# A gate with key sums on half the array, strided fills in place of mask tables, and a new written order of all steps

## The chip, the cores and the metric

The kernel runs on one core of one Trainium2 chip. Its metric is the device time of one execution in microseconds (us). The core has five engines that run side by side and wait for each other by semaphores: TensorE (PE, with weight loads shown apart as PEld), VectorE (DVE), ScalarE (ACT), GpSimd (POOL) and SyncE (SP), which here does nothing but issue DMAs. Each engine takes its own instructions strictly in the order in which the program wrote them, so one that waits holds up all that stand behind it on that engine. PSUM, where TensorE writes, is used as four places of 4 KB per partition.

## The reference, cut to what matters

Two layers follow one another. The first is a block-sparse attention over 4 batches, 8 heads, 768 positions and 64 features. The second mixes its output by a two-dimensional Fourier transform (real part) and ends in a normalised two-layer network.

```python
k_rep = k.reshape(B, H, n_blocks, block, D).mean(axis=3)      # 12 blocks of 64 keys
gate_scores = np.einsum('bhsd,bhnd->bhsn', q, k_rep)
gate_scores = np.where(causal, gate_scores, -1000000000.0)
top_idx = np.argsort(gate_scores, axis=-1)[..., -top_k:]      # top_k = 3
# a query may see the keys of its three best blocks and of its own block, causally
scores = np.where(mask, scale * (q @ k.T), -1000000000.0)
x = softmax(scores) @ v                                       # heads side by side: (4, 768, 512)
mixed = np.real(np.fft.fft(np.fft.fft(x, axis=1), axis=2))
u = x + mixed
un = (u - mean(u)) / sqrt(var(u) + 1e-6)
out = u + maximum(un @ w_ch1, 0.0) @ w_ch2                    # 512 -> 2048 -> 512
```

## The kernel before, in words

The work is cut into 16 pairs of heads (four pairs to a batch) and then into four batches. The text `ORDER` names every step by letters and indices, and a loop at the end of the kernel (L767) writes the steps' instructions in exactly that order. Every engine's queue is therefore `ORDER` with the other engines' steps left out. Nothing is reordered later.

**Loads** (SP's queue): `Lk`, `Lq`, `Lv` fetch a pair's keys, queries and values into `nat` buffers (three for k, three for q, two for v); pairs 7 to 15 have k and q fetched by four DMAs in blocks of 32. `LF`, `LT`, `Lc`, `Li` fetch Fourier and indicator tables. `W:c` and `X:c` fetch the network's weights and are issued on POOL's queue.

**Attention of a pair P.** For P below 7 (`NX`), `tk` and `tq` transpose k and q on PE into PSUM; from 7 on, `kb` and `qc` transpose 32x32 blocks on DVE. `ks` (DVE, L306) sums keys by block into `kr12`; `kh` (DVE, recorded at the helper of all two-operand steps, L221) multiplies these sums by a table `half` of 0 and 1, so that each of the two heads has sums on its own 64 partitions and zeros on the other 64. `kc` (ACT) and `qc` (DVE), `qs` (POOL) make the copies that the score matmuls read. The **gate** is `g` (PE, block scores: L347 or L354), `gt` (DVE: turn the scores, then shut out blocks that lie ahead: for P below 7 a minimum with the table `lim`, else three fills), `gx` (DVE: the eight largest of each row), `gl:P,0` (DVE: 1 where a block is below the third largest), `gl:P,1` (DVE: multiply by the table `oth` or `oth2`, which holds -60000 or, for the own block, 0) and `gm` (DVE: turn back, giving `mt`). For P from 7 on, `K` (POOL, ten instructions) copies `mt` beside the queries. `s` (PE, six tiles 0 to 5) makes the scores with the mask added, by the indicator rows `indz` in matmuls of their own (L433) for P below 7, or within the same matmul of 96 rows (L426). `e` (ACT, L443) takes the exponential, `d` (POOL, L449) clears the upper triangle of the diagonal part, `vc` (POOL) casts v, `v` (PE, L461) multiplies by v, `x` (DVE, L472 and L221) divides by the sum.

**Fourier part and network of a batch b.** `fs`, `fd`, `f` (DVE) fold the batch's four pairs; `pg` (POOL) holds POOL until the folds are done. `y` (PE), `ty` (ACT) and `tr` (DVE), `m` (PE, three), `u` (DVE, L578, adds x), `xu` (ACT, centres) follow. The result is turned by `xt` (PE) and `un` (DVE, L602) for batch 0 and by six DMAs on SP's queue for the others (`un`, L605). Then come 16 steps `w` (PE, L641 and L643, first layer) with `r` (ACT or, every fourth, DVE), and 12 steps `c` (PE, L668) with `o` (DVE, L680) and `od` (SP, the output). `bn`, `nv` (DVE) and `nr` (POOL) make the norm.

**PSUM and other buffers.** All PSUM tiles share one tag with four buffers, which are handed out in turn: a new tile waits until the tile four allocations earlier has been read. `nat`, `q32`, `mt`, `pt` and `u_b` rotate in the same way.

Before the first `w` there is no network work with which to fill PE; from then on `w` and `c` steps of one batch stand between the attention steps of the next.

Of the kernel before, what the change touches and what calls it, by code (L numbers as in the profile page):

```python
# [11 lines left out]
FP = mybir.dt.float32  # L12
# [3 lines left out]
NEG = -60000.0  # L16
# [12 lines left out]
def _consts_np():  # L29
# [22 lines left out]
    oth = np.where(np.arange(9)[:, None] + 3 != nn, NEG, 0.0)[None].repeat(128, 0)  # L52

    lim = np.where(nn[None, 4:8] > np.arange(3, 7)[:, None], -3e38, 3e38)
    lim = lim.reshape(1, 16).repeat(128, 0).astype(np.float32)
# [6 lines left out]
    own = 2 * np.arange(5)[None, :] + 2 + (p // 64)[:, None]  # L62
    oth2 = np.zeros((128, 5, 2, 16), np.float32)
    oth2[:, :, :, 0:NB] = np.where(own[:, :, None, None] != nn, NEG, 0.0)
# [3 lines left out]
    return dict(FS=fs.astype(np.float16), FD=fd.astype(np.float16),  # L68
                oth=oth.reshape(128, 108).astype(np.float16),
                lim=lim,  # L70
                indc=indc.reshape(128, 24).astype(np.float16),
                oth2=oth2.reshape(128, 160).astype(np.float16),
# [40 lines left out]
Lk:1 Lq:1 Lk:2 Lq:2 Lq:3 Lk:3 tk:0 ks:0 kh:0 iz:1 iz:0 tq:0 kc:0 qc:0 g:0 tq:1 gt:0 gx:0 gl:0,0  # L113
gl:0,1 gm:0 qc:1 tk:1 kc:1 tk:2 kc:2 ks:1 qs:0 qs:1 Lq:4 Lv:0 Lk:4 Lv:1 kh:1 s:0,1 ks:2 s:0,3 tq:2
qc:2 g:1 kh:2 e:0,1 s:0,0 s:0,5 gt:1 s:0,4 s:0,2 tk:3 e:0,3 e:0,5 g:2 gx:1 gl:1,0 Lq:5 Lk:5 gl:1,1
gm:1 s:1,4 tq:3 s:1,3 e:0,0 tq:4 gt:2 tk:4 e:0,4 ks:3 qc:3 gx:2 gl:2,0 s:1,0 kh:3 qc:4 gl:2,1 s:1,1
e:0,2 g:3 ks:4 e:1,4 gm:2 Lv:2 d:0,3 qs:2 d:0,4 d:0,2 vc:0 vc:1 d:0,0 d:0,1 d:0,5 Lv:3 Lq:6 LF:0
Lq:7 Lk:6 Lk:7 LT:0 v:0 s:1,5 s:2,4 e:1,3 kc:3 tq:5 e:1,0 s:2,5 s:2,2 e:1,1 gt:3 kc:4 gx:3 gl:3,0
kh:4 x:0 e:1,5 g:4 s:1,2 s:2,3 e:2,4 e:2,5 qc:5 gl:3,1 e:2,2 gt:4 e:1,2 tk:5 gx:4 gm:3 ks:5 e:2,3
s:2,1 e:2,1 qs:4 qs:3 vc:2 d:1,4 d:2,5 qs:5 d:1,0 d:1,3 d:1,5 d:1,2 d:1,1 fs:0,0 kh:5 gl:4,0 fs:0,1  # L120
gl:4,1 v:1 x:1 s:3,1 s:2,0 s:3,4 g:5 kc:5 s:3,3 e:3,1 e:3,4 s:3,0 qc:7 gm:4 e:2,0 tq:6 e:3,0 s:3,5
e:3,5 e:3,3 gt:5 s:3,2 s:4,1 e:3,2 fs:1,1 gx:5 fs:1,0 gl:5,0 Lv:4 Lq:8 Lk:8 Lv:5 Lc:0 d:3,1 d:2,1
d:2,2 d:3,4 d:2,0 d:3,5 d:3,0 d:2,3 d:2,4 vc:3 d:3,2 d:3,3 gl:5,1 kb:7 v:2 e:4,1 kc:7 gm:5 ks:7 v:3
s:4,5 e:4,5 s:4,0 qc:6 x:2 s:5,4 e:5,4 s:5,5 s:4,4 x:3 s:5,2 s:4,3 s:5,0 tk:6 e:5,5 fs:2,0 kh:7
fs:3,1 fs:3,0 fs:2,1 fd:3,0 fd:2,0 fd:2,1 fd:3,1 f:0,2 f:0,0 f:0,1 y:0,0 e:4,4 ks:6 f:0,3 y:0,1
e:5,2 s:5,3 e:5,0 e:4,0 tr:0,0 e:4,3 tr:0,1 m:0,2 kc:6 ty:0,0 g:7 ty:0,1 kh:6 m:0,1 u:0,2 g:6 u:0,1
# [3 lines left out]
r:0,6 w:0,12 e:6,1 w:0,11 w:0,2 qc:8 ks:8 gm:7 kb:9 kh:8 g:8 r:0,12 s:6,0 r:0,11 s:6,5 w:0,0 e:6,4  # L130
r:0,2 w:0,5 w:0,8 w:0,1 e:6,5 ks:9 r:0,5 gt:8 gx:8 gl:8,0 kh:9 gl:8,1 w:0,3 bn:0,5 gm:8 qc:9 bn:0,3
Lq:10 Lk:10 Lv:6 Lq:11 d:6,1 K:7 qs:7 d:6,4 d:5,2 d:5,4 d:6,3 X:0 d:5,3 d:6,5 d:5,5 vc:5 d:5,1 Li:0
Lv:7 Lq:12 Lv:8 Lv:9 s:7,3 v:5 r:0,8 r:0,0 r:0,3 r:0,1 e:6,0 bn:0,1 x:5 s:7,2 e:7,3 w:0,15 g:9 s:7,4
e:7,2 w:0,9 e:7,4 fs:5,0 s:7,5 gt:9 s:7,1 w:0,13 r:0,15 r:0,9 s:7,0 kb:10 gx:9 ks:10 qc:10 kh:10
fs:4,1 w:0,10 gl:9,0 fs:5,1 g:10 w:0,14 e:7,1 e:7,5 e:7,0 w:0,7 bn:0,4 gt:10 bn:0,0 bn:0,2 gx:10
gl:9,1 gm:9 r:0,7 r:0,13 w:0,4 gl:10,0 gl:10,1 nv:0 d:6,0 qs:8 K:8 X:1 d:7,4 d:6,2 d:7,0 d:7,2 d:7,5
vc:7 d:7,1 vc:6 qs:9 d:7,3 K:9 nr:0 v:6 kc:8 s:8,5 s:8,2 r:0,14 s:8,4 r:0,10 kc:9 v:7 r:0,4 c:0,0,0
s:9,0 s:8,3 s:9,1 e:8,5 c:0,0,1 s:9,3 x:6 x:7 c:0,1,0 s:8,0 e:8,2 fs:6,1 c:0,1,1 fs:7,1 fs:7,0
fd:7,0 fs:4,0 fs:6,0 fd:6,0 qc:11 fd:7,1 fd:6,1 f:1,2 f:1,0 f:1,3 f:1,1 y:1,0 tr:1,0 e:8,4 e:8,3
o:0,1 e:9,1 kc:10 e:9,3 y:1,1 c:0,4,0 e:9,0 e:8,0 c:0,5,0 ty:1,1 s:8,1 o:0,0 Lv:10 Lv:11 Lk:11 Lq:13  # L140
od:0,1 od:0,0 Lq:14 Lk:12 ty:1,0 s:9,5 e:9,5 tr:1,1 kb:11 ks:11 kh:11 m:1,1 m:1,0 g:11 e:8,1 u:1,1
# [658 lines left out]
```

## Time and profile before

| what | value |
|---|---|
| median of 3 runs | 293.21 us (292.3 to 293.62) |
| the profiled execution: span from first to last instruction | 290.3 us |
| PE / DVE / ACT / POOL busy | 274.3 / 203.0 / 164.4 / 113.2 us |
| TensorE clock granted | 1.000 of full speed |
| bytes read / written | 28.63 MB / 6.29 MB |

The profile states the profiled execution by its span alone. The three runs lie 2.0 to 3.3 us above that span, which is the time around the first and the last instruction together with the difference between executions; a change in the span is carried over to the time as it stands.

How to read it: an engine's busy time says how much of the span it worked, not whether it set the end. The view by stretches gives the busy time of each engine in a stretch. The view of waits says who waited for whom. The chain that ended last goes from the last instruction back to whatever released each step. In views of one tile or line the three durations are the least, the median and the largest in nanoseconds.

### The profile page before, as it was taken

How to read it: one execution, taken by the hardware profiler on the slowest of the kernel's cores; microseconds unless marked ns; L12 is line 12 of the kernel's file. 1: busy time of each engine (PE TensorE's matmuls, PEld its weight loads, DVE VectorE, ACT ScalarE, POOL GpSimd, SP SyncE). 2: the span in 40 equal slices, each digit the busy share in tenths (PEclk: the TensorE clock that was granted, in tenths of full speed). 3: DMA queues.
4: the chain of work that ended last, by engine and by line, in shares of the span. 5: the costliest groups of instructions: out<-in, count | busy, mean ns of one | idle time of the engine just before them, and what ended most of it. 6: DMA issues, size and time to landing. Idle time of an engine off the chain costs nothing.

```text
span 290.3 us, 6581 instructions
## 1 busy us (share of the span) xinstructions
PE 274.3 (94%) x2525; PEld 167.7 (58%) x2525; DVE 203.0 (70%) x606; ACT 164.4 (57%) x205; POOL 113.2 (39%) x286
## 2 busy tenths in 40 slices
PE   7696976899999999999999999999999999999995
PEld 3554664575656665565576457646766654656443
DVE  2899988999789988689988668609691559202122
ACT  3676878877579666579888505687143231263000
POOL 2246470614988815845760489414400001100000
PEclk9999999999999999999999999999999999999999
DMA  9999999899999399964900004541000024000034
GB/s 200 267 236 263 172 215 178 140 180 162 154 189 205 76 183 212 130 131 117 213 17 2 0 0 148 109 92 73 2 2 0 36 76 108 0 2 0 0 147 181
DMA packets 121423, 33.52 MB, mean 115 GB/s; under 512 B 114160, under 2 KB 118192, under 8 KB 121392
## 3 DMA queue, kind: packets, MB, share of 16 engines
q1 hardware_dynamic: 115728, 28.47, 46.0%
q0 software_dynamic: 3664, 4.19, 9.2%
q10 hardware_dynamic: 2000, 0.44, 0.7%
q8 instruction: 20, 0.33, 0.5%
q14 instruction: 11, 0.09, 0.1%
HBM read 28.63 MB, written 6.29 MB: 120 GB/s over the span
## 4 chain that ended last, share of the span: by engine, by line
PE 79%; DVE 13%; ACT 5%; issue 2%; DMA 1%; DVEq 0%; ACTq 0%
PE c L668 27%; PE h L641 19%; PE h L643 10%; PE sc L426 7%; PE av L461 4%; ACT pt L443 4%; DVE u L578 2%; PE yp L531 2%; DVE kr L306 2%; DVE q L328 2%; PE warmps L705 1%; PE sc L421 1%; DVE mx L378 1%; PE c L660 1%; PE g L354 1%
## 5 line engine op out<-in xcount | busy, mean ns | idle before, releaser
L443 ACT ACTIVATE pt<-sc 128x1024 f16<-128x1024 f32 (+1 forms) x96 | 83.5, 918 | 26.1 <-PE sc L426 14.6
L641 PE MATMUL h<-unT,w 128*128 128x512 f16 x256 | 84.5, 379 | 0.0
L668 PE MATMUL c<-w_sb,hT 128*128 128x512 f16 x368 | 83.0, 379 | 0.2 <-ACT pt L443 0.2
L643 PE MATMUL h<-unT,w 128*128 128x256 f16 x256 | 69.7, 272 | 0.0
L449 POOL TENSOR_SCALAR_AFFINE_SELECT pt<-pt 128x256 f16<-128x256 f16 x96 | 38.5, 424 | 68.0 <-ACT pt L443 45.9
L668 PEld LDWEIGHTS <-hT 128*128 128x128 f16 x368 | 35.7, 98 | 40.6 <-issue 0.7
L653 ACT ACTIVATE hT<-h 128x768 f16<-128x768 f32 x48 | 37.4, 809 | 34.7 <-PE h L643 34.6
L641 PEld LDWEIGHTS <-w 128*128 128x128 f16 x256 | 25.0, 98 | 29.5 <-issue 0.7
L680 DVE SCALAR_TENSOR_TENSOR u<-c,rs,u 128x512 f32<-128x512 f32 (+1 forms) x25 | 17.3, 724 | 29.9 <-PE c L668 25.6
L651 DVE TENSOR_SCALAR hT<-h 128x768 f16<-128x768 f32 x16 | 15.2, 948 | 19.4 <-PE h L643 19.4
L643 PEld LDWEIGHTS <-w 128*128 128x128 f16 x256 | 25.0, 98 | 3.9
L426 PE MATMUL sc<-qk 96*128 96x512 f16 (+3 forms) x144 | 26.0, 306 | 0.1
L224 POOL TENSOR_SCALAR_AFFINE_SELECT qk<-q 64x768 f16<-64x768 f32 (+1 forms) x25 | 21.0, 843 | 12.8 <-DVE q L328 12.1
L590 ACT ACTIVATE x<-u,nm 128x512 f16<-128x512 f32 x24 | 16.0, 714 | 16.3 <-DVE nm L584 16.2
L224 POOL TENSOR_SCALAR_AFFINE_SELECT qk<-mt 32x160 f16<-32x160 f16 x72 | 23.0, 340 | 2.6 <-DVE mt L398 0.9
L461 PEld LDWEIGHTS <-pt 128*128 128x128 f16 x672 | 22.2, 97 | 2.8 <-issue 1.1
L461 PE MATMUL av<-v,pt 128*128 128x65 f16 x672 | 23.0, 193 | 0.5 <-ACT pt L443 0.3
L421 PE MATMUL sc<-qk 64*128 64x512 f16 (+3 forms) x112 | 14.9, 306 | 5.4 <-ACT pt L443 3.2
L578 DVE SCALAR_TENSOR_TENSOR u<-mx,x 128x512 f32<-128x512 f32 x24 | 15.6, 685 | 5.2 <-PE mx L565 5.2
L224 POOL TENSOR_SCALAR_AFFINE_SELECT v<-nat 128x768 f16<-128x768 f32 x16 | 14.7, 920 | 8.6 <-DMA nat<-in_v_dram 8.6
L426 PEld LDWEIGHTS <-qk 96*128 96x128 f16 x144 | 12.7, 97 | 8.6 <-issue 0.9
L544 ACT CAST ty<-yp 128x772 f16<-128x772 f32 x8 | 8.0, 1036 | 16.7 <-PE yp L531 16.4
(98 smaller groups left out, 349.2 us busy)
## 6 DMA issues: line engine op xcount, KB each, us to landing
nat<-in_v_dram SPq DMA_DIRECT2D x16, 384.0 KB, 5.0
out_dram<-u SPq DMA_DIRECT2D x23, 256.0 KB, 2.5
nat<-in_q_dram SPq DMA_DIRECT2D x36, 96.0 KB, 3.0
nat<-in_k_dram SPq DMA_DIRECT2D x36, 96.0 KB, 3.1
nat<-in_k_dram SPq DMA_DIRECT2D x13, 192.0 KB, 3.3
nat<-in_q_dram SPq DMA_DIRECT2D x13, 192.0 KB, 3.5
w_sb<-in_moe_w_ch_dram POOLq DMA_DIRECT2D x2, 1024.0 KB, 9.8
w<-in_moe_w_ch_dram POOLq DMA_DIRECT2D x2, 768.0 KB, 9.4
```

The lines of the kernel that those rows point to most:

```text
L224: nc.gpsimd.affine_select(out=out, in_=in_, pattern=[[0, i] for i in n], base=0, channel_multiplier=0, compare_op=ALU.is_ge, fill=0.0)
L421: nc.tensor.matmul(ps[:, e, co:co + q1 - q0], qk[hs[e], 1, XW(P), 128 * jt:128 * jt + 128], qk[hs[e], 0, XW(P), q0:q1], start=(co == 0), s ...
L426: nc.tensor.matmul(ps[:, e, co:co + q1 - q0], qk[0:96, e, 1, 128 * jt:128 * jt + 128], qk[0:96, e, 0, q0:q1], start=True, stop=True)
L443: nc.scalar.activation(out=d["pt"][:, o:o + 2 * n].rearrange("p (e c) -> p e c", e=2), in_=d["sc", i][:, :, 0:n], func=AF.Exp, scale=0.125)
L449: nc.gpsimd.affine_select(out=dg, in_=dg, pattern=[[0, 2], [1, 128]], base=0, channel_multiplier=-1, compare_op=ALU.is_ge, fill=0.0)
L461: nc.tensor.matmul(av[:, e, 66 * st:66 * st + 65], pt[:, co:co + 128], vv[:, e, jt, 0:65], start=(cnt == 0), stop=(cnt == 20))
L578: nc.vector.scalar_tensor_tensor(out=u_b[:, k2, :].rearrange("p (m two) -> p two m", two=2), in0=mps[:, k2, :].rearrange("p (two m) -> p t ...
L641: nc.tensor.matmul(hp[:, 0:512], w1s, unT[:, dt, 0:512], start=(dt == 0), stop=(dt == NDT - 1))
L643: nc.tensor.matmul(hp[:, 512:768], w1s, unT[:, dt, 512:768], start=(dt == 0), stop=(dt == NDT - 1))
L653: nc.scalar.activation(out=hT, in_=hp, func=AF.Relu)
L668: nc.tensor.matmul(c_ps[b, g[0]][:, st - g[0], :], h_t[b, it][:, 128 * st:128 * (st + 1)], w2_sb[:, it, :], start=(it == 0), stop=(it == N ...
L680: nc.vector.scalar_tensor_tensor(out=o, in0=ps, scalar=st_t[b][1][:, st:st + 1], in1=o, op0=ALU.mult, op1=ALU.add)
```

## The change

Six things are done together.

1. **Key sums (pairs 0 to 6).** `kh` is dropped for these pairs. `ks` writes `kr_s` directly; its second head axis is gone. The gate's matmul reads only the 64 partitions of its head, `kr_s[hs, :]` against `qq[hs, ...]`, so each matmul uses half the array's rows.
2. **Block bound (pairs 0 to 6).** The minimum with `lim` becomes two strided fills of `gt` with -3e38.
3. **Own block.** The product with `oth` or `oth2` is dropped. A new step `go` fills the own block's score with 3e38 after `gx` (one fill for P below 7, two from 7 on), so that it is never below the third largest. `gl` is now one instruction.
4. **Masks.** They are 0 and 1. The -60000 moves into the indicator tables `indc` and `ind`.
5. **Tables.** `lim`, `oth` and `oth2` and their three loads (two on ACT's queue at the start, one in `Lc` on SP's) are gone.
6. **Order and places.** `ORDER` is written anew from start to end, and steps carry `@n`. PSUM tiles and the rotating buffers have one tag for each place n with one buffer each. A tile now waits for the last tile of its place, whatever was allocated in between.

```diff
     for g in range(4):
         for n in range(NB):
-            indc[g, n, g % 2, n] = 1.0
+            indc[g, n, g % 2, n] = NEG
...
-        ind[e, 16 * e:16 * e + NB] = nn[:, None] == (s[None, :] // 64)
+        ind[e, 16 * e:16 * e + NB] = np.where(nn[:, None] == (s[None, :] // 64), NEG, 0.0)
...
-    psump = ctx.enter_context(tc.tile_pool(name="psum", bufs=4, space=bass.MemoryType.PSUM))
+    psump = ctx.enter_context(tc.tile_pool(name="psum", bufs=1, space=bass.MemoryType.PSUM))
...
+    place = [0]
+
     def pst(shape, name, dtype=FP):
-        return psump.tile(shape, dtype, tag="ps", name=name)
+        return psump.tile(shape, dtype, tag=f"ps{place[0]}", name=name)
...
-    kr_s = [ctile([128, 2, 32], FP, f"kr{i}") for i in range(NSLOT)]
+    kr_s = [ctile([128, 32], FP, f"kr{i}") for i in range(NSLOT)]
...
     def a_sums(P):
         ps = pairs[P]["tp", 1]
-        pairs[P]["kr12"] = kr12 = spool.tile([128, NB], FP, tag="kr12", name=f"kr12_{P}")
+        if P < NX:
+            kr12 = kr_s[P % NSLOT][:, 0:NB]
+        else:
+            pairs[P]["kr12"] = kr12 = spool.tile([128, NB], FP, tag="kr12", name=f"kr12_{P}")
...
             for c in range(4):
+                hs = slice(64 * (c // 2), 64 * (c // 2) + 64)
                 nc.tensor.matmul(g[32 * c:32 * c + 32, :].rearrange("p (b i) -> p b i", i=32),
-                                 kr_s[slot][:, c // 2, :], qq[:, :, c % 2, :], start=True, stop=True)
+                                 kr_s[slot][hs, :], qq[hs, :, c % 2, :], start=True, stop=True)
...
             nc.vector.transpose(out=gt, in_=d["g"])
-            x = gt.rearrange("p (b n) -> p b n", n=32)[:, 0:4, 4:8]
-            tt(x, x, lim, ALU.min)
+            for c, n in ((4, 4), (6, 2)):
+                nc.vector.memset(gt[:, c:c + 33 * n].rearrange("p (b n) -> p b n", n=33)[:, :, 0:2],
+                                 -3e38)
             return
...
-        if j == 0:
-            tt(l, gt, mx[:, :, 2:3].to_broadcast([128, 9 if P < NX else 10, NB]), ALU.is_lt)
-        else:
-            tt(l, l, o, ALU.mult)
+        tt(l, gt, mx[:, :, 2:3].to_broadcast([128, 9 if P < NX else 10, NB]), ALU.is_lt)
+
+    def g_own(P):
+        gt = pairs[P]["gt"]
+        if P < NX:
+            nc.vector.memset(gt[:, 3:3 + 33 * 8 + 1:33], 3e38)
+            return
+        for h in range(2):
+            nc.vector.memset(gt[64 * h:64 * h + 64, 2 + h:2 + h + 170].rearrange(
+                "p (b c) -> p b c", c=34)[:, :, 0:17:16], 3e38)
...
         for x in ORDER.split():
+            x, _, at = x.partition("@")
+            place[0] = int(at or 0)
             n, a = x.split(":")
             WORK[n](*[int(i) for i in a.split(",")])
```

Of the order, the stretch around the first `w` before, then the new one there and at the hand-over to batch 1:

```diff
-s:4,2 gt:6 e:5,3 m:0,0 s:5,1 xu:0,2 e:4,2 xu:0,1 xt:0,1 gx:6 e:5,1 u:0,0 xu:0,0 Lk:9 Lq:9 W:0 W:1
-d:4,0 pg:0 vc:4 d:4,4 d:5,0 qs:6 d:4,3 d:4,1 W:2 d:4,2 d:4,5 gl:6,0 gl:6,1 v:4 un:0,1 gm:6 s:6,3
-gt:7 xt:0,0 xt:0,2 s:6,1 s:6,4 x:4 e:6,3 s:6,2 e:6,2 un:0,0 un:0,2 gx:7 gl:7,0 gl:7,1 kb:8 w:0,6
...
+e:5,4 s:5,5@2 f:0,0 e:5,5 s:5,0@1 e:4,1 tk:6@2 f:0,1 f:0,2 e:5,0 y:0,0@0 Lk:9@2 ks:6 f:0,3 kc:6
+y:0,1@1 tr:0,0 pg:0 d:4,4 Lk:8@1 vc:6 g:6@2 tr:0,1 ty:0,0 qs:6 qc:7@0 ty:0,1 m:0,2@0 W:1 gt:6
+Lv:5@1 e:5,2 m:0,0@1 d:5,0 u:0,2@0 d:5,5 Lc:0 m:0,1@2 d:5,4 W:2 g:7@3 u:0,0@1 xu:0,2 vc:4 xt:0,2@0
+d:4,5 d:5,1 u:0,1@2 xu:0,0 d:4,1 d:4,3 xt:0,0@1 d:4,2 gx:6 d:4,0 xu:0,1 v:4@2 go:6 un:0,2 gl:6 kc:7
+un:0,0 xt:0,1@0 gm:6@2 s:6,3@1 un:0,1 e:6,3@0 gt:7 s:6,4@0 w:0,9@3 x:4 Lk:10@0 e:6,4 vc:5 s:6,1@1
...
+kc:10 d:9,3 m:1,2@0 d:9,1 d:9,4 kc:12 c:0,2,0@1 kh:11 d:9,5 u:1,1@4 d:8,2 K:10 kc:11 Lk:13@0
+u:1,2@1 g:11@3 c:0,3,0 gt:11 d:8,1 xu:1,2 d:8,0 Lq:12@2 s:10,3@0 bn:1,3 d:8,4 v:8@3 vc:9 xu:1,0
+pg:1 vc:10 c:0,3,1 x:8 e:10,3@0 Lk:14@1 d:9,2 xu:1,1 gx:11 v:9@0 go:11 o:0,3 Lv:12@1 kh:12 gl:11
+s:10,5@3 c:0,2,1 gm:11@3 e:10,5 un:1,2 x:9 K:11 kb:14 c:0,5,0 qc:12@1 Lv:11@0 vc:12 un:1,0 s:11,4@3
+o:0,2 s:10,1@0 e:11,4@1 c:0,5,1 qs:12 bn:1,0 e:10,1 un:1,1 fs:9,0 s:10,0@1 d:10,5 qc:13@0 s:11,0@3
```

More of the change, by code (lines that the diff above doesn't have):

```diff
@@ L231 @@
     id16 = ctile([128, 128], F16, "id16")
-    oth = ctile([128, 9, NB], F16, "oth")
-    lim = ctile([128, 4, 4], FP, "lim")
     indc = ctile([128, 24], F16, "indc")
@@ L267, in load @@
         if who == 2:
[L268 removed]
+            t = apool.tile([128, 2 * NST, 64], FP, tag=f"nat2{place[0]}", name=f"nat2_{P}", bufs=1)
             eng.dma_start(t, src[b, 2 * hp:2 * hp + 2].rearrange("e (st p) d -> p (e st) d", p=128))
@@ L271, in load @@
             return
-        t = apool.tile([128, NST, 2, 64], FP, tag=f"nat{who}", name=f"nat{who}_{P}", bufs=3)
+        t = apool.tile([128, NST, 2, 64], FP, tag=f"nat{who}{place[0]}", name=f"nat{who}_{P}", bufs=1)
         nat[P, who] = t
@@ L322, in a_q32 @@
     def a_q32(P):
-        q32 = apool.tile([128, S], FP, tag="q32", name=f"q32_{P}")
+        q32 = apool.tile([128, S], FP, tag=f"q32{place[0]}", name=f"q32_{P}", bufs=1)
         pairs[P]["q32"] = q32
@@ L383, in g_less @@
         if P < NX:
-            gt, l, o = d["gt"].rearrange("p (b n) -> p b n", n=32)[:, :, 0:NB], lt[:, :, 0:NB], oth
+            gt, l = d["gt"].rearrange("p (b n) -> p b n", n=32)[:, :, 0:NB], lt[:, :, 0:NB]
             d["lt"] = lt.rearrange("p b n -> p (b n)")
@@ L387, in g_less @@
             gt = d["gt"][:, 0:160].rearrange("p (j n) -> p j n", n=16)[:, :, 0:NB]
-            l, o = [t.rearrange("p b e n -> p (b e) n")[:, :, 0:NB] for t in (ltb, oth2)]
+            l = ltb.rearrange("p b e n -> p (b e) n")[:, :, 0:NB]
             d["lt"] = ltb.rearrange("p b e n -> p (b e n)")
-        if j == 0:
-            tt(l, gt, mx[:, :, 2:3].to_broadcast([128, 9 if P < NX else 10, NB]), ALU.is_lt)
-        else:
-            tt(l, l, o, ALU.mult)
+        tt(l, gt, mx[:, :, 2:3].to_broadcast([128, 9 if P < NX else 10, NB]), ALU.is_lt)
[7 more added lines that the diff above has]
+                "p (b c) -> p b c", c=34)[:, :, 0:17:16], 3e38)
     def g_back(P):
         d = pairs[P]
-        d["mt"] = apool.tile([128, 288 if P < NX else 160], F16, tag="mt", name=f"mt_{P}", bufs=4)
+        d["mt"] = apool.tile([128, 288 if P < NX else 160], F16, tag=f"mt{place[0]}", name=f"mt_{P}", bufs=1)
         nc.vector.transpose(out=d["mt"], in_=d["lt"])
@@ L440, in s_exp @@
         if "pt" not in d:
-            d["pt"] = apool.tile([128, PT_W], F16, tag="pt", name=f"pt_{P}")
+            d["pt"] = apool.tile([128, PT_W], F16, tag=f"pt{place[0]}", name=f"pt_{P}", bufs=1)
         o, n = SC_OFF[i], sum(q1 - q0 for (_, q0, q1) in SC_TILES[i])
@@ L569, in m_u @@
         mps, x_b = m_ps[b, kp], x_t[b]
-        u_t[b, kp] = u_b = bpool.tile([128, 2, DM], FP, tag="u_b", name=f"u{kp}_{b}", bufs=5)
+        u_t[b, kp] = u_b = bpool.tile([128, 2, DM], FP, tag=f"u_b{place[0]}", name=f"u{kp}_{b}", bufs=1)
         if b not in st_t:
@@ L690, in consts_first @@
             src = (q, k)[who]
-            t = apool.tile([128, NST, 2, 64], FP, tag=f"nat{who}", name=f"nat{who}_0", bufs=3)
+            t = apool.tile([128, NST, 2, 64], FP, tag=f"nat{who}{place[0]}", name=f"nat{who}_0", bufs=1)
             nat[0, who] = t
@@ L719, in consts_first @@
         nc.scalar.dma_start(indc, dr["indc"].ap())
-        nc.scalar.dma_start(lim, dr["lim"].ap().rearrange("p (b n) -> p b n", n=4))
-        nc.scalar.dma_start(oth, dr["oth"].ap().rearrange("p (b n) -> p b n", n=NB))
     def blocks(w):
```

140 lines of the change are left out of this document (64 added, 76 removed).

## The prediction

> **What bounds the kernel now.** I read the page's busy shares and slices first, then the busy time by stretches, then the waits, then the timeline at the first network step.
>
> ```profile
> span 290.3 us, 6581 instructions
> PE 274.3 (94%) x2525; PEld 167.7 (58%) x2525; DVE 203.0 (70%) x606; ACT 164.4 (57%) x205; POOL 113.2 (39%) x286
> ...
> PE   7696976899999999999999999999999999999995
> ...
> DVE  2899988999789988689988668609691559202122
> ...
> GB/s 200 267 236 263 172 215 178 140 180 162 154 189 205 76 183 212 130 131 117 213 17 2 0 0 148 109 92 73 2 2 0 36 76 108 0 2 0 0 147 181
> ```
>
> PE is full from about slice 9 on and not before; there DVE is. The cut lies at the first `w`, after the last copy of batch 0's turned rows. The chain's last pieces mark where PE ends.
>
> ```profile
> 64.47 0.68 DVE L602 COPY unT<-xt 128x1024 f16<-128x1024 f16 x1
> ...
> 65.35 0.39 PE L641 MATMUL h<-unT,w 128*128 128x512 f16 x1
> ```
>
> ```profile
> 285.38 1.76 PE c L660 x16
> ...
> 287.16 0.48 DVE u L680
> ```
>
> With those cuts the stretches read (the first two columns are the stretch and its length, then busy time by engine, clock, DMA share, GB/s):
>
> ```profile
> core 0: us, PE busy (x) PEld busy (x) DVE busy (x) ACT busy (x) POOL busy (x), PEclk, DMA share, GB/s
> 0.00:6.57 6.57, 5.17 (x20) 2.59 (x21) 1.36 (x11) 1.93 (x3) 1.66 (x17) 1.00 0.87 191
> 6.57:65.20 58.63, 47.51 (x751) 33.41 (x749) 54.51 (x181) 45.19 (x56) 24.55 (x47) 1.00 1.05 208
> 65.20:287.20 222.00, 221.61 (x1762) 131.67 (x1756) 146.71 (x418) 117.25 (x147) 87.02 (x222) 1.00 0.43 89
> 287.20:290.30 3.10, 0.00 (x0) 0.00 (x0) 0.45 (x1) 0.00 (x0) 0.00 (x0) 1.00 0.30 106
> ```
>
> So there are two kernels in one. From 6.57 to 65.20 DVE works 54.51 of 58.63 us and PE has 11.1 us to spare. From 65.20 to 287.20 PE works 221.61 of 222.00; the one wait of PE there is
>
> ```profile
> PE c L668 <- ACT pt L443: 0.2, 1, 0.2
> ```
>
> and DVE's few waits in the first part (after its start) are
>
> ```profile
> DVE gt L361 <- PE g L347: 1.2, 2, 0.9
> DVE kr L306 <- PE tp L297: 0.8, 1, 0.8
> ```
>
> The consequence carries the whole sum: DVE work taken away before the first `w` shortens the span until another engine takes over, at 47.51 us of PE or 45.19 of ACT; DVE work taken away later is worth nothing, since PE's 221.61 us cover it. If PE ever waited there, that cover would be gone.
>
> **The gate on DVE, first part.** All seven gates of pairs 0 to 6 come before the first `w` in both orders. What goes (least, median, largest ns):
>
> ```profile
> L221 DVE TENSOR_TENSOR kr<-kr,half x7: 175/183/1416, 7.6 to 54.0; 128x24 f32<-128x24 f32 x7
> ```
>
> ```profile
> L221 DVE TENSOR_TENSOR gt<-gt,lim x7: 174/304/407, 10.0 to 58.7; 128x16 f32<-128x16 f32 x7
> ```
>
> ```profile
> L221 DVE TENSOR_TENSOR ltb<-ltb,oth x9: 215/223/489, 66.2 to 170.5; 128x120 f16<-128x120 f16 x9
> L221 DVE TENSOR_TENSOR lt<-lt,oth x7: 200/216/217, 11.3 to 61.2; 128x108 f16<-128x108 f16 x7
> ```
>
> ```profile
> L221 DVE TENSOR_TENSOR kr<-kr,half 128x24 f32<-128x24 f32 x7 | 2.9, 412 | 0.2
> ...
> L221 DVE TENSOR_TENSOR gt<-gt,lim 128x16 f32<-128x16 f32 x7 | 1.9, 277 | 0.2
> ...
> L221 DVE TENSOR_TENSOR lt<-lt,oth 128x108 f16<-128x108 f16 x7 | 1.5, 212 | 0.1
> ```
>
> By least durations 7 x (175+174+200) ns = 3.8 us, by medians 7 x (183+304+216) = 4.9, by group totals 2.9+1.9+1.5 = 6.3. What comes is 7 x 3 strided fills; the trace has such fills, on other pairs:
>
> ```profile
> L368 DVE MEMSET gt<- x9: 67/67/67, 62.7 to 164.4; 64x10 f32 x9
> ```
>
> 21 x 67 ns = 1.4 us, and not less than nothing. I take medians and full fills, -3.5 us (ends -2.4 and -6.3): one long `kr` of 1416 ns is an accident of its moment and not seven times to be had. [...]
>
> For pairs 7 to 15 one product (223 ns) gives way to two fills (134): 9 x 89 ns = 0.8 us of DVE work, nearly all behind the first `w`, worth 0; PE covers it.
>
> **What the new order moves over the first `w`.** On DVE, `gt:7` and `x:4` stood ahead of the last `un:0` and now stand behind it:
>
> ```profile
> L221 DVE TENSOR_TENSOR x<-av,rcp 128x768 f16<-128x768 f32 x16 | 15.3, 957 | 0.6
> ...
> L472 DVE RECIPROCAL rcp<-av 128x12 f32<-128x12 f32 x16 | 3.7, 229 | 5.3 <-PE av L461 5.2
> ...
> L366 DVE STREAM_TRANSPOSE gt<-g 128x160 f32<-128x160 f32 x9 | 3.0, 337 | 3.0 <-PE g L354 3.0
> ```
>
> 0.957+0.229+0.337+0.2 (three fills) = 1.7 us earlier; nobody in the first part waits for either. On PE, `s:6,1` and `s:6,2` go behind the first `w`, where their time is paid in full. One such tile, start to start of what follows it:
>
> ```profile
> 62.35 0.39 PE L421 MATMUL sc<-qk 64*128 64x384 f16 x4
> ...
> 62.58 0.36 PE L433 MATMUL sc<-mt,indz 64*128 64x160 f16 x8
> ...
> 62.88 1.07 PE L597 MATMUL xt<-id,x 128*128 128x128 f16 x16
> ```
>
> 0.53 us, two of them: +1.0.
>
> **POOL in front of the last `un:0`.** In the new order POOL stops at `pg:0` until `f:0,3` is done, with ten `d`, two `vc`, `qs:6`, `W:1` and `W:2` queued behind it, and `v:4` needs the last of these `d`; `xt:0,1`, hence `un:0,1`, stands behind `v:4` on PE.
>
> ```profile
> L449 POOL TENSOR_SCALAR_AFFINE_SELECT pt<-pt 128x256 f16<-128x256 f16 x96 | 38.5, 424 | 68.0 <-ACT pt L443 45.9 <-issue 21.4
> ...
> L224 POOL TENSOR_SCALAR_AFFINE_SELECT v<-nat 128x768 f16<-128x768 f32 x16 | 14.7, 920 | 8.6 <-DMA nat<-in_v_dram 8.6
> ```
>
> ```profile
> L461 PE MATMUL av<-v,pt 128*128 128x65 f16 x672 | 23.0, 193 | 0.5 <-ACT pt L443 0.3 <-DVE u L578 0.2
> ```
>
> ```profile
> L735 POOL DMA_DIRECT2D w<-in_moe_w_ch_dram x3: 746/757/954, 41.9 to 55.4; - x3
> ...
> DMA to landing us min/median/max: 7.9/8.0/10.9
> ```
>
> 10 x 0.424 + 2 x 0.920 + some 0.9 for `qs:6` + 2 x 0.757 = 8.5 us, then 23.0/16 = 1.4 for `v:4` and, as an estimate, 0.4 for `xt:0,1`: 10.3. Between the same two points DVE has two `tr`, `qc:7`, `gt:6`, three `u`, the rest of gate 6 and two `un`, which I estimate at 10 us from their places before. I put the hold at 0.4, ends 0 and 2. `W:1`, which the first `w` reads, is issued about 2.5 us behind `pg:0` and lands 8 to 10.9 later, so it arrives with the last `un:0` too; I add nothing, and up to 2 at the far end.
>
> **The half-array key sums on PE.** Eight instructions of one gate, start to start of the next kind:
>
> ```profile
> 8.77 0.69 PE L347 MATMUL g<-q,kr 128*32 128x288 f32 x8 [1.92 <-DVE q L328]
> ...
> 9.39 0.44 PE L297 MATMUL tp<-id,nat 128*128 128x128 f32 x2
> ```
>
> 0.62 us for eight of some 0.4 us each: the four column parts already overlap, so halving the rows gives them nothing. I take 0.
>
> **Loads.** Three table loads fewer: nobody waited for them, worth 0, as the value loads and `nat` places hide it. By the new order one q load fewer net goes ahead of the first `w` (`Lq:8`, `Lq:9` later, `Lv:6` earlier); SP stays just ahead, as before.
>
> **The long part.** The work on PE is the same. What can change is waiting. The turning DMAs stand on SP's queue behind loads and outputs:
>
> ```profile
> L605 SPq DMA_TRANSPOSE unT<-x x18: 1206/1217/2942, 117.2 to 242.6; - x18
> ...
> DMA to landing us min/median/max: 2.4/2.5/5.0
> ```
>
> Six take 6 x 1.217 = 7.3 us of the queue. For batch 1 they now follow `Lk:13` (waits for `kc:10`), `Lq:12`, `Lk:14` (waits for `kc:12`) and `Lv:12` (waits for `vc:9`). Counting PE work in the new order from `vc:9` to `w:1,1` I find about 12 us against 7.3 + 1.3 landing beyond the last issue + 0.4 = 9, so a reserve of a few us at the first and, for batches 2 and 3 by the same count, of about one or less. Three hand-overs and the fixed places: +0.8, ends 0 and 6. The tail, one `o` and one `od` behind the last `c`, stays 3.1.
>
> **Sum.** First `w` at 65.35 - 3.5 - 1.7 + 0.4 = 60.5 (DVE's old idle of 4.1 us kept). Then -4.8 + 1.0 + 0.8 = -3.0: span 287.3. The profiled span stands 2.9 below the median of 293.21; the same distance gives 290.2. PE would then work about 46.5 us in some 54 between 6.57 and the first `w`, ACT 45, which leaves room.
>
> **Rivals.**
> (1) *The long part gives it back (slower).* One mechanism: SP works strictly in order, and the six turning DMAs of a batch sit behind a load whose buffer comes free late. Place: the first `w` of batches 1, 2 and 3; price: each us of lateness beyond the reserve is a us of idle PE, with nothing to put in its stead. It decides from 3.0 + 0.8 = 3.8 us in all. Two us at each of three hand-overs give 287.3 + 5.2 = 292.5 span, 295.4. For: reserves of one us, against a queue step that took up to 2942 ns. Against: the present order has the same queue and PE waits 0.2.
> (2) *DVE is not what is left; the loads are (no change).* 208 GB/s x 58.63 us = 12.2 MB are moved before the first `w`; the new order wants about 0.4 MB less, 11.8 MB. At the same rate that takes 56.7 us, so the first `w` comes at 63.3, 1.9 earlier; less 1.0 and 0.8 that is nothing: 293.1. For: DMA share 1.05. Against: slices of 263 and 267 GB/s.
> (3) *Halves of the gate matmul run after each other.* If two row halves that write one PSUM tile cannot overlap, each gate takes 0.62 us more, 7 x 0.62 = 4.3; DVE waits for `g` in few places, so a third reaches it, 1.4: 291.6. [...]
> (4) *All of it arrives.* Group totals and no waits: -6.3 + 1.4 - 1.7 + 1.0 = -5.6, 287.6.
>
> **How the numbers follow.** My forecast, 290.2 (own range 288.5 to 292), has 0.50; rival 1 0.22, rival 2 0.12, rival 3 0.08, rival 4 0.08. This kernel's three runs spread by 0.45%, so 0.5% (1.5 us, below 291.7 or above 294.7) is about what can be told from no change. Faster: 0.45 of the forecast, 0.08 of rival 4, 0.04 of 3, 0.03 of 2 = 0.60; slower: 0.20 of rival 1 and 0.02 of 2 = 0.22; the rest, 0.18, is same. The range 287.8 to 295.0 leaves out about half of rivals 1 and 4.
>
> **What would show it.** First `w` near 60.5 and DVE still over 0.9 busy before it: the gate term. Fills of some 67 ns: right. A gate's eight matmuls at 0.62: rival 3 wrong. PE's waits after the first `w` under 1.5 us in all: the long part right; waits of PE on turning DMAs or on DVE's reads of places: rival 1. A first `w` at 63 with PE or DVE waiting for loads: rival 2. My prediction is wrong most easily where PE waits behind the first `w`, which no row of the present trace can price.

## The result and the profile after

| | median | runs |
|---|---|---|
| before | 292.79 us | 292.3 to 293.62 |
| after | 300.63 us | 300.18 to 301.29 |

The changed kernel is slower: the ratio is 1.0263, 95% interval 1.0228 to 1.0298. The forecast was 290.2, and its range ended at 295.0. The page of the changed kernel:

```profile
span 299.6 us, 6592 instructions
...
PE 276.6 (92%) x2525; PEld 167.9 (56%) x2525; DVE 194.4 (65%) x615; ACT 165.6 (55%) x205; POOL 113.0 (38%) x286
...
PE   7689878787998999998999999999999998999994
...
GB/s 164 218 203 216 172 240 174 134 223 134 79 129 197 181 135 225 128 186 114 176 35 57 0 0 124 22 114 78 2 2 0 105 55 89 105 2 0 0 122 125
...
q1 hardware_dynamic: 115584, 28.43, 50.7%
...
nat<-in_k_dram SPq DMA_DIRECT2D x13, 192.0 KB, 4.6
nat<-in_q_dram SPq DMA_DIRECT2D x13, 192.0 KB, 4.8
```

The same rows of the kernel before, from its page:

```profile
q1 hardware_dynamic: 115728, 28.47, 46.0%
...
nat<-in_k_dram SPq DMA_DIRECT2D x13, 192.0 KB, 3.3
nat<-in_q_dram SPq DMA_DIRECT2D x13, 192.0 KB, 3.5
```

DVE lost 203.0 - 194.4 = 8.6 us of work, so the change does take work from it. But the load queue (q1) moves the same 28.4 MB and takes 50.7% of a longer span in place of 46.0%: 151.9 us of the 16 engines in place of 133.5. The view by stretches, cut at the first `w` of the changed kernel (columns as in the prediction):

```profile
6.57:65.00 58.43, 46.67 (x736) 33.63 (x736) 49.02 (x178) 45.16 (x56) 26.05 (x51) 1.00 1.09 196
65.00:72.20 7.20, 5.49 (x58) 3.26 (x55) 6.97 (x24) 4.89 (x7) 1.54 (x3) 1.00 1.10 166
72.20:80.00 7.80, 7.80 (x75) 4.25 (x72) 4.12 (x9) 3.56 (x4) 5.36 (x14) 0.78 0.50 82
80.00:295.80 215.80, 212.12 (x1655) 124.77 (x1652) 132.41 (x396) 110.50 (x137) 78.47 (x202) 1.00 0.46 87
```

In the first part DVE works 49.02 us where it worked 54.51, and yet the first `w` comes at 65.0, as before. Neither DVE nor PE fills that stretch. PE's waits (whole span):

```profile
PE tp L292 <- DMA nat<-in_q_dram: 3.5, 3, 1.7
PE tp L292 <- DMA nat<-in_k_dram: 3.3, 3, 1.4
...
PE av L467 <- POOL v L222: 1.7, 1, 1.7
PE g L353 <- DVE q L324: 1.4, 1, 1.4
...
PE h L647 <- DMA unT<-x: 1.0, 1, 1.0
PE h L649 <- DMA unT<-x: 0.9, 1, 0.9
```

The first two are new: 6.8 us of waits for key and query loads ahead of the first `w`. The loads are slow from the first one on, before any order of steps can matter. The transfer view for the first 16 us, in 40 slices of 0.4 us, of the kernel before and then of the changed kernel:

```profile
GB/s 0 0 0 0 8 235 259 277 284 289 284 287 277 274 269 272 284 287 261 239 239 274 271 263 261 273 284 274 273 265 275 267 252 283 271 278 277 271 268 275
```

```profile
GB/s 0 0 0 0 10 152 188 261 286 280 237 218 219 213 218 209 211 213 214 219 218 218 216 219 219 216 216 218 219 216 220 216 220 218 216 218 218 218 220 215
```

The kernel before holds about 270 GB/s. The changed one falls to between 209 and 220 and stays there, flat and without a gap. The pieces themselves took longer, though not all of them: of the 55296 pieces of 256 bytes in each trace 5% took 24 ns or more before the change and 28% after it, while the median stayed at 18 ns.

Behind the first `w` the lateness goes on. POOL's timeline of the changed kernel:

```profile
52.87 0.18 POOL L525 COPY gone<-fg 1x4 f16<-1x4 f16 x1 [10.84 <-DVE fg L522]
...
70.66 0.90 POOL L222 TENSOR_SCALAR_AFFINE_SELECT v<-nat 128x768 f16<-128x768 f32 x1 [10.00 <-ACT hT L659]
```

The row at 70.66 is `vc:5`. The view names ACT as its releaser, but its load `Lv:5`, issued at 56.0, had only landed at 70.6. `v:5` on PE waited 1.7 us for it. Behind that gap the granted clock averages 0.78 over 7.8 us (0.50 from 73.2 to 76.4 us), which costs PE, as an estimate, another 7.8 x 0.22 = 1.7. That the gap brought the drop on is not shown.

### The profile page after: what moved, and what is told of

The parts are those of the page before. It is cut to its first block, busy times and chain, and to the rows that moved or that the text cites. A ratio compares the mean times of both kernels' runs of the same rounds, so it can differ in the third digit from the quotient of the medians.

```text
span 299.6 us, 6592 instructions
## 1 busy us (share of the span) xinstructions
PE 276.6 (92%) x2525; PEld 167.9 (56%) x2525; DVE 194.4 (65%) x615; ACT 165.6 (55%) x205; POOL 113.0 (38%) x286
## 3 DMA queue, kind: packets, MB, share of 16 engines
q1 hardware_dynamic: 115584, 28.43, 50.7%
## 4 chain that ended last, share of the span: by engine, by line
PE 64%; DMA 13%; DVE 10%; POOL 3%; SPq 3%; ACT 3%; issue 2%; DVEq 0%; ACTq 0%; POOLq 0%
PE c L674 18%; PE h L647 18%; PE h L649 9%; PE av L467 6%; DMA nat<-in_k_dram 5%; PE sc L432 4%; DMA nat<-in_q_dram 3%; ACT pt L449 2%; SPq L277 2%; DMA nat<-in_v_dram 2%; POOL qk L222 2%; DMA unT<-x 2%; DVE u L584 2%; PE yp L537 1%; PE c L666 1%
## 5 line engine op out<-in xcount | busy, mean ns | idle before, releaser
L647 PE MATMUL h<-unT,w 128*128 128x512 f16 x256 | 86.0, 383 | 1.0 <-DMA unT<-x 1.0
L674 PE MATMUL c<-w_sb,hT 128*128 128x512 f16 x368 | 83.9, 379 | 0.0
L659 ACT ACTIVATE hT<-h 128x768 f16<-128x768 f32 x48 | 38.1, 810 | 38.6 <-PE h L649 38.4
L455 POOL TENSOR_SCALAR_AFFINE_SELECT pt<-pt 128x256 f16<-128x256 f16 x96 | 37.0, 412 | 35.2 <-ACT pt L449 28.8
L432 PE MATMUL sc<-qk 96*128 96x512 f16 (+3 forms) x144 | 26.8, 306 | 0.0
L219 POOL TENSOR_TENSOR t<-vr,rs 128x6 f32<-128x6 f32 x12 | 2.7, 222 | 42.8 <-DVE rs L627 42.2
L432 PEld LDWEIGHTS <-qk 96*128 96x128 f16 x144 | 13.3, 97 | 9.3 <-issue 0.3
L292 PE MATMUL tp<-id,nat 128*128 128x128 f32 x84 | 11.8, 279 | 7.1 <-DMA nat<-in_q_dram 3.5
```

What stands on the lines that cost most here:

```text
L432: nc.tensor.matmul(ps[:, e, co:co + q1 - q0], qk[0:96, e, 1, 128 * jt:128 * jt + 128], qk[0:96, e, 0, q0:q1], start=True, stop=True)
L455: nc.gpsimd.affine_select(out=dg, in_=dg, pattern=[[0, 2], [1, 128]], base=0, channel_multiplier=-1, compare_op=ALU.is_ge, fill=0.0)
L647: nc.tensor.matmul(hp[:, 0:512], w1s, unT[:, dt, 0:512], start=(dt == 0), stop=(dt == NDT - 1))
L659: nc.scalar.activation(out=hT, in_=hp, func=AF.Relu)
L674: nc.tensor.matmul(c_ps[b, g[0]][:, st - g[0], :], h_t[b, it][:, 128 * st:128 * (st + 1)], w2_sb[:, it, :], start=(it == 0), stop=(it == N ...
```

## The experiments

Three theories were on the table after the first comparison. **L:** the new order issues its loads too late. **G:** the new gate itself costs. **P:** the new places and waits hold the first part up. A fourth, **A**, came from the addresses of the buffers in the built programs. The change drops `lim` (64 bytes per partition), `oth` (224) and `oth2` (320), and shrinks three `kr_s` by 128 each: 992 bytes. All that is laid out behind them moves down by as much. In the kernel before, the load buffers `nat0` and `nat1` start at 96768 and 87552, multiples of 256; in the changed kernel they start 32 past one (992 = 4 x 256 - 32). The loads consist of pieces of 256 bytes, 64 float32; those of keys and queries from pair 7 on have 128.

**e1, e2: the two halves of the change alone.** e1 is the kernel before with the new gate and the old order; e2 the changed kernel with the old gate and its tables.

In e1 (e2 is the reverse of it, in the changed kernel):

```diff
-    oth = ctile([128, 9, NB], F16, "oth")
-    lim = ctile([128, 4, 4], FP, "lim")
-    oth2 = ctile([128, 5, 2, 16], F16, "oth2")
-    kr_s = [ctile([128, 2, 32], FP, f"kr{i}") for i in range(NSLOT)]
+    kr_s = [ctile([128, 32], FP, f"kr{i}") for i in range(NSLOT)]
...
-    "gx": g_max, "gl": g_less, "gm": g_back
+    "gx": g_max, "go": g_own, "gl": g_less, "gm": g_back
```

> Only the new gate (half-array key sums, fills, 0/1 masks, one compare), in the old order with the old rotating buffers; every gl pair becomes go and gl at the place of the first, kh of pairs 0 to 6 is dropped. Theory L (the new order issues and receives its loads too late, the gate itself is good): first w near 61, DVE being the bound there, time 288 to 290.5. Theory G (the gate itself costs, because two row halves write one PSUM tile or the fills are slow): first w at 65 or later, time 293 or more, eight gate matmuls over 0.9 us.

> Only the new order and places, with the old gate put back (kh right after ks, gl in two steps at the place of gl, no go; the three tables are loaded again). Theory L: the order carries the loss, so it is as slow as the whole change or slower by part of the 5 us of DVE work that comes back: 300 to 305, PE waiting 5 to 8 us for q and k loads before the first w. Theory G: the order is not to blame, 289 to 294.

e1 took 297.84 us against 292.9 (ratio 1.0159, 1.0064 to 1.0254) and e2 297.81 (1.0124, 1.0054 to 1.0195). Each half alone loses 4 to 5 us, and e2 lies in neither of the ranges expected for it, so none of the theories does for both. e1 shows slow loads (share of q1 52.1%) and its first `w` at 68.8; e2 has them fast (45.1%). With the old gate the new order has 55.31 us of DVE work ahead of a first `w` at 65.3, so nothing is gained there, and it adds waits of PE; e2's view of waits:

```profile
PE xt L603 <- ACT x L596: 3.5, 3, 2.0
PE g L353 <- DVE kr L227: 2.2, 3, 1.0
PE g L360 <- DVE q L332: 1.7, 1, 1.7
```

e1 speaks against L, since the old order is slow too. That the loads are slow in e1 and fast in e2 goes with the dropped tables, not with the order.

**e3, e4: wider loads, and the kernel before again.** e3 is the whole change with its q, k and v loads written in runs of 1536 or 3072 bytes. It brings other rows to each partition, so it computes on permuted inputs; the amount of work is the same.

```diff
-            src[b, 2 * hp + e].rearrange("(st p) d -> p st d", p=128)
+            src[b, 2 * hp + e].rearrange("(p st) d -> p (st d)", p=128)
```

> The whole change, but all loads of q, k and v fetch the same bytes in runs of 1536 or 3072 bytes in place of 256 or 128 (rows and features of q, k and v come out permuted, so this computes the attention of other rows; every instruction of the five engines stays). Theory L: loads land earlier, PE no longer waits for them, first w near 60 and time 287 to 292. Rival P (fixed places and waits among engines hold the first part, the late loads only fill time that would be lost anyway): first w stays at 63 to 65 and time above 296.

> The kernel before, unchanged, to see its loads on the same chip. If loads are slower on this chip than in the first profile, its first four loads land at 4.7 to 6.5 us as in the profile after; if they are slower because of the changed kernel, they land at 4.1 to 5.9 us as before. First w at 65.4 plus or minus 0.3, one time near 293.

e3 took 293.49 us (1.0031, 1.0007 to 1.0055), 7 less than the change, with q1 at 33.6%, no wait of PE for loads and the first `w` at 62.0. So the loads carry the loss, and theory P falls. e3 doesn't say why they are slow: it has fewer pieces as well as longer ones. e4, the unchanged kernel, gave 293.5 with q1 at 45.9%.

**e5, e6: the load buffers put back to a multiple of 256.** Two unused tiles, nothing else, in the changed kernel (e5) and in e1 (e6).

```diff
+    ctile([128, 152], FP, "pad0")   # 608 bytes, behind half
+    ctile([128, 96], FP, "pad1")    # 384 bytes, ahead of dummy
```

> The changed kernel with 992 bytes per partition of unused tiles in place of the tables that the change drops and of the kr_s that it shrinks, so that the load buffers nat0 and nat1 stand at a multiple of 256 bytes in a partition again, as before the change (without the two unused tiles they stand 32 bytes past one). No instruction is added or taken. Theory A, the loads are slow because their 256-byte pieces no longer start at a multiple of 256 bytes: the first four loads land at 4.1 to 4.8, 4.8 to 5.2 and 5.8 to 6.1 us as in the kernel before, one 384 KB load again takes about 1.6 us and not 1.8, the share of the load queue falls from 50.7% to 45 to 46%, PE's waits for nat in the first part (some 17 us of lines in all) mostly go, the first w comes at 61 to 63 instead of 65.0, and the time falls from 300.6 to 294 to 297 (what is left is the late W:1, W:2 and Lv:5 behind the first w). Theory G, the new gate's own instructions cost the time: the time stays at 299 to 302 and the queue's share above 50%. Theory L, the new order issues the loads too late: the share of the queue may fall, but the first w stays at 64 to 66 and the time at 298 or above. [...]

> The new gate in the order and the places of the kernel before (as e1), with the same 992 bytes of unused tiles, so that the load buffers stand at a multiple of 256 bytes. Theory A: e1's loss (297.8 against 292.9) was the loads' alone; the time falls to 288 to 292, under the kernel before, since DVE does 3.5 us less ahead of the first w, which comes at 61 to 64 (68.8 in e1). Theory G: e1's loss is the gate's, and the time stays at 296 to 299. If it comes at 292 to 294, the loads made e1's loss and the gate's gain on DVE is worth nothing at the path.

e5 took 292.7 us (ratio 1.0001, 0.9978 to 1.0025): 7.9 us less than the changed kernel, by two tiles that nothing reads, and 1.3 less than the lowest time expected. The stretch of 7 to 16 us moved 266 GB/s, only 4% of the pieces of 256 bytes took 24 ns or more, and the first `w` came at 60.05, so theory L falls with the order unchanged; the stretch up to it, and the row of that `w` in the timeline:

```profile
6.57:60.00 53.43, 46.26 (x737) 33.63 (x735) 48.84 (x179) 44.95 (x56) 26.01 (x51) 1.00 1.05 217
```

```profile
60.05 0.39 PE L649 MATMUL h<-unT,w 128*128 128x512 f16 x1
```

e6 took 291.13 us (0.9945, 0.9917 to 0.9972), 6.7 less than e1 and below the kernel before. Theory G falls: with its loads in place the new gate gains.

**e7, e8: the kernel before, shifted.** One unused tile of 32 (e7) or 64 bytes (e8) behind its last constant.

```diff
+    ctile([128, 8], FP, "pad1")     # e8: [128, 16]
     dummy = ctile([128, 1], FP, "dummy")
```

> The kernel before with one unused tile of 32 bytes per partition behind its last constant, so that all buffers behind it, the load buffers among them, stand 32 bytes further on; nothing else is touched. Theory A: the loads take 1.8 us each instead of 1.6, the first land at 4.7, 5.8 and 6.5 us, the load queue's share rises from 46% to 50 to 52%, PE waits for nat or the DVE chain is starved, and the time rises from 292.9 to 296 to 301. Theories G and L: nothing of the gate or of the order is in it, so 292 to 294.

> The kernel before with an unused tile of 64 bytes per partition instead of 32. Two forms of theory A: if a piece of 256 bytes has to start at a multiple of 256, this is as slow as the shift by 32 (296 to 301, share of the load queue 50 to 52%); if a multiple of 64 is enough, it is as before (292 to 294, 46%). [...]

e7 took 300.49 us (1.0232, 1.0175 to 1.0289), the changed kernel's time to 0.1 us with no line of the change in it. e8 took 297.73 (1.0152, 1.0115 to 1.0188). The stretch of 7 to 16 us, where the kernel before has 268 GB/s, in e7 and in e8:

```profile
7.00:16.00 9.00, 5.86 (x66) 4.35 (x70) 6.54 (x22) 5.70 (x7) 1.73 (x3) 1.00 1.39 216
```

```profile
7.00:16.00 9.00, 5.50 (x66) 4.03 (x67) 6.82 (x21) 5.68 (x7) 1.65 (x2) 1.00 1.38 216
```

The shift by 64 lowered the rate as much as the one by 32 (216 GB/s in both). That its time is nonetheless 2.8 us shorter I can't explain; the two intervals just overlap. In the profiled executions the granted clock drops twice in e7 and once in e8 (0.989 and 0.994 in the mean), but no run separates the two.

**e9, e10: the key and query buffers alone.** The shift goes ahead of `nat0`, `nat1` and `q32`, and is filled up to 256 behind them, so that every other buffer keeps its place within 256 bytes.

```diff
+    ctile([128, 8], FP, "pad1")     # e10: [128, 32]
...
     def a_q32(P):
+        if P == 0:
+            apool.tile([128, 56], FP, tag="padq", name="padq", bufs=1)   # e10: [128, 32]
```

> The kernel before with 32 bytes of unused tile ahead of the buffers that the key and query loads write (nat0, nat1) and q32, and 224 bytes behind these, so that they alone stand 32 bytes past a multiple of 256 and everything behind them (value load buffers, x, unT, pt, zeros) keeps its place within 256 bytes. If it is the place of the load buffers that costs (theory A in its narrow form): 297 to 301, as with all buffers shifted (300.5), share of the load queue 50 to 52%. If it is another buffer (a rival: x or unT under the turning transfers, or the engines' reads and writes of shifted tiles): 292 to 294 and 46%.

> As e9 with 128 bytes ahead and 128 behind. If a 256-byte piece has to start at a multiple of 256: slow, 296 to 301, share of the load queue 50 to 52%. If the shifts by 32 and 64 cost by their own distance and 128 is a boundary that suffices: 292 to 294 and 46%. [...]

e9 took 298.37 us (1.0203, 1.0181 to 1.0225): of e7's 2.3% these buffers carry 2.0. e10 took 295.19 (1.0103, 1.0082 to 1.0123), between the two ranges expected for it. Rows of the transfer view (KB each, median us to landing) of the kernel before, then of e9, then of e10:

```profile
nat<-in_q_dram SPq DMA_DIRECT2D x36, 96.0 KB, 3.0
nat<-in_k_dram SPq DMA_DIRECT2D x36, 96.0 KB, 3.1
```

```profile
q1 hardware_dynamic: 115728, 28.47, 52.0%
...
nat<-in_q_dram SPq DMA_DIRECT2D x36, 96.0 KB, 4.2
nat<-in_k_dram SPq DMA_DIRECT2D x36, 96.0 KB, 3.9
nat<-in_k_dram SPq DMA_DIRECT2D x13, 192.0 KB, 5.2
```

```profile
q1 hardware_dynamic: 115728, 28.47, 47.9%
...
nat<-in_q_dram SPq DMA_DIRECT2D x36, 96.0 KB, 3.0
nat<-in_k_dram SPq DMA_DIRECT2D x36, 96.0 KB, 2.8
nat<-in_k_dram SPq DMA_DIRECT2D x13, 192.0 KB, 4.5
```

With a shift by 128 the early loads, whose pieces have 256 bytes, stay slow (216 GB/s in the stretch of 7 to 16, as in e9). The later ones of 96 KB, whose pieces have 128 bytes, land as in the kernel before (2.8 and 3.0 us). The key and query loads of the kernel before, e7, e8, e9 and e10 can be put in one statement: they were slow where pieces of theirs lie across a multiple of 256 (216 GB/s in the stretch of 7 to 16 at 32, 64 and 128, and 3.9 and 4.2 us to landing for 96 KB at 32) and not where none does (268 GB/s before the change, and 2.8 and 3.0 us for 96 KB at 128). Pieces of 128 bytes at 128 don't lie across one; at 32 every second one does.

**e11, e12: two versions that might beat both.** e11 is e6 with the value buffers too at a multiple of 256 (they stand at 128 past one before the change). e12 is e5 with that, and with the read of query pair 9 earlier on DVE.

The edit of e11 to e6, in `a_q32`, and that of e12 to the order of e5 (beside 64 and 192 bytes ahead of its two value buffers):

```diff
+        if P == 0:
+            apool.tile([128, 32], FP, tag="padq", name="padq", bufs=1)
```

```diff
-X:1 go:8 kh:10 gl:8 w:0,4@3 qc:9@0
+X:1 qc:9@0 go:8 gl:8 kh:10 w:0,4@3
```

> e6 (new gate, old order, unused tiles) with 128 more bytes of unused tile ahead of the value load buffers nat2, which stand at 128 past a multiple of 256 in e6 and in the kernel before; they come to a multiple of 256. If 128 costs as 32 does: 16 value loads of 384 KB at about 0.2 us of the queues each (1.8 against 1.6 us), of which eight lie ahead of or beside the first part: the load queue's share falls from 46.4% to about 45%, the first w comes 0.5 to 1.5 us sooner and the time is 289.5 to 291. If 128 costs nothing: 291.1 as e6.

> e5 (the whole change with its load buffers at multiples of 256) with the value load buffers put there too, and on DVE the transpose of query pair 9 ahead of the compares of pair 8 and the halving of pair 10 behind them: in e5 PE waited 1.43 us for that transpose at 82, which DVE began only at 82.35 though its data had landed at 78.0. If that wait falls with no new one: 292.7 less 1.4, with the value loads up to 1 less, so 290 to 291.5. If it only moves to another step (the compares of pair 8 late for its scores), 292 to 293.

e11 took 290.53 us (0.994, 0.9917 to 0.9963), the lowest median of all. Against e6 the share of q1 fell from 46.4 to 45.2% and the first `w` came at 62.6, not 64.1, but the two intervals overlap: that the value buffers' place brings time is not shown. Nor is the 1.5 us of first `w`, for in e6's profiled execution the granted clock drops ahead of it (0.97 in the mean, 1.00 in e11). What is shown is that the loads gain: 5.5% of the pieces of 256 bytes took 24 ns or more in e6, 0.3% in e11, where every load buffer is at a multiple of 256 (4% in e5, 2% in e12). e12 took 291.88 (1.0005, 0.9976 to 1.0034), no better than e5 by its interval; its runs spread from 290.5 to 294.5. The executions with a mean granted clock of 0.999 or 1.000 took 290.5 to 292.1, the others 292.8 or more. In the profiled one, the longest and one of these others, the wait for query 9 is gone, that of `xt` is 3.5 us in place of e5's 1.9, and one on `gt` is new:

```profile
PE xt L604 <- ACT x L597: 3.5, 4, 2.0
...
PE h L648 <- DVE gt L367: 1.1, 1, 1.1
PE h L650 <- DMA unT<-x: 0.9, 1, 0.9
```

**All of it in one table** (median us; they come from several sessions, in which the kernel before took 292.1 to 292.9):

| | old gate | new gate |
|---|---|---|
| old order, loads at a multiple of 256 | 292.8 (before) | 291.1 (e6) |
| old order, 32 bytes past it | 300.5 (e7) | 297.8 (e1) |
| new order, loads at a multiple of 256 | 297.8 (e2) | 292.7 (e5) |
| new order, 32 bytes past it | not run | 300.6 (the change) |

The 32 bytes cost 6.7 to 7.9 us in each of the three pairs. The new gate gains 1.7 to 5.1. The new order loses 1.6 or 2.8 with the new gate, 5.0 with the old.

## Why the prediction was wrong

**The step that failed is the one on loads:** "Three table loads fewer: nobody waited for them, worth 0" and "SP stays just ahead, as before". The three transfers were indeed worth nothing. What I left out is that the tables also took up room: without them, and with the smaller `kr_s`, every buffer behind them moves, and the load buffers come to stand 32 bytes past a multiple of 256. I counted every instruction and not one address. The term is +7.9 us (300.6 less e5's 292.7), three quarters of the miss of 10.4.

The rate does not go by the distance: from 268 GB/s it fell to 216 at 32 (e7), at 64 (e8) and at 128 (e10) alike. What makes a shifted piece take longer, no trace of this case shows.

**DVE bounds the first part: right where the loads come in time; the gate alone brings less.** Predicted was DVE work of 54.51 - 3.5 - 1.7 = 49.3 us ahead of the first `w`; it was 49.02 after and 48.84 in e5. Predicted was a first `w` at 60.5; e5 has 60.05. That execution is the shortest of e5's ten; e12's, with a drop of the clock ahead of it (0.97 in the mean), has its first `w` at 62.1. And e6, the new gate in the old order with its loads in place, splits the sum:

```profile
6.57:64.10 57.53, 48.70 (x750) 34.29 (x748) 49.67 (x182) 45.37 (x56) 24.96 (x47) 0.97 1.07 210
```

```profile
DVE q L313 <- DMA nat<-in_q_dram: 2.1, 1, 2.1
```

The gate took 54.51 - 49.67 = 4.8 us off DVE, or 3.4 against e4, the kernel before once more, whose DVE worked 53.0 us up to its first `w`; 3.5 were taken. The new order took 0.8 more (to 48.84), where 1.7 were taken. But the gate alone brought the first `w` only 1.2 us forward in e6 (with a drop of the clock ahead of it) and 2.7 in e11: in the old order DVE now waits for a query load, 2.1 us in e6 and 1.4 in e11. The order alone brought nothing (e2, 65.3, a drop ahead of it too, 0.97 in the mean). So the 5.3 us of e5 need both, and the prediction, which adds up one term for each, got them right only in the sum. The fills are as cheap as taken; from the view of the gate's tile in the changed kernel (least, median, largest ns):

```profile
L362 DVE MEMSET gt<- x14: 62/64/65, 10.9 to 56.2; 128x8 f32 x7, 128x4 f32 x7
```

**POOL's hold: none seen, where 0.4 was taken.** POOL stood 10.84 us at `pg:0` (the first row of its timeline above), and its `d` and `vc` behind it, up to `vc:4` for `v:4`, held up no row of PE's waits ahead of the first `w`, here or in e5. `W:1` went out at 55.0 and landed at 63.2, ahead of a first `w` at 65.0; nobody waited for it.

**Half-array key sums at 0: right, rival 3 wrong.** The eight matmuls, on 64 rows now, take 0.69 us as they did on 128; from the changed kernel's timeline of PE:

```profile
9.33 0.69 PE L346 MATMUL g<-q,kr 64*32 64x288 f32 x8
```

**The long part: under-sized.** Taken were +1.0 for moved work and +0.8 for waits, 1.8 over the old 221.85 (65.35 to 287.20). In e5 PE works from 60.05 to 286.29, 226.2 us, +4.4. PE has 47.51 - 46.26 = 1.25 less work in the first part, so that much more behind it; its waits there are

```profile
PE g L355 <- DVE q L326: 1.4, 1, 1.4
PE h L651 <- DMA unT<-x: 1.0, 1, 1.0
PE av L469 <- POOL pt L457: 0.4, 1, 0.4
```

2.8 us, within the ends of 0 to 6; some 0.3 I can't place. The tail is 3.8 us where I had 3.1. So e5's span is 287.3 - 0.4 + 2.6 + 0.7 = 290.2 (profiled: 290.1): the first part gives 5.3 us, and the long part and the tail give 5.1 back. Without the addresses the prediction would have missed by 2.5 us and still been too hopeful: no change, not faster.

**The rivals.** Rival 1 (turning DMAs late) exists with 1.0 us in e5 and 1.9 after, not the 6 that it needed. Rival 2 named the right resource and the wrong reason: it held the rate at 208 GB/s and asked how much was moved, which gave 63.3; the rate itself fell to 196, and the first `w` came at 65.0. Rival 4's full gain came nowhere. My last sentence said that waits behind the first `w` would make me wrong "most easily"; they were the smaller part.

## What to carry to other kernels

A table that is dropped or a tile that shrinks moves all that is laid out behind it, so a diff that deletes constants also changes the start address of the load buffers. Before costing such an edit, work out where these buffers stand modulo 256 in both kernels, and pin them at a multiple with an unused tile, which here brought 7.9 us back (e5). In the trace the sign was a load rate that is lower and flat from the first loads on (217 GB/s in the stretch of 7 to 16 us in place of 268), with the same 28.4 MB in nearly as many packets (115584 and 115728); judge the rest of the change only with the loads in the same place.

## What the runs showed of the hardware

- In the stretch of 7 to 16 us loads in 256-byte pieces ran at 262 to 286 GB/s into key and query buffers at a multiple of 256 (268 before the change; e2, e5, e6, e11, e12) and at 216 to 218 into buffers 32, 64 or 128 bytes past one (the changed kernel, e1, e7 to e10). Shifted by 32, the kernel before lost 2.3% (e7). Loads of 96 KB in pieces of 128 bytes lost nothing at a shift of 128 (e10, 2.8 and 3.0 us to landing where it was 3.1 and 3.0) and 0.8 and 1.2 us at 32 (e9). With the slower rate went a larger share of slow pieces: 25 to 30% of the 256-byte pieces took 24 ns or more in the kernels with shifted key and query buffers, 2 to 6% in those without, 0.3% in e11, and the median was 18 ns in all. Whether only the boundary at 256 matters, or a smaller one too for shorter pieces, no run separates.
- After a gap of 1.7 us on PE at 70 us the granted clock averaged 0.78 over the next 7.8 us, though PE was busy throughout. Two gaps as long did not have that behind them: after one of 1.71 us that ends at 39.9 in the same trace and after one of 1.92 that ends at 8.8 in the kernel before it was 1.00.
